# Moving a pair of second products behind scores and P@V in a fused attention and feed-forward kernel, with weights loaded in fewer slots

## The chip, the cores and the metric

One core of a Trainium2 chip. The time is device microseconds of one execution, median of several runs. PE is TensorE, DVE is VectorE, ACT is ScalarE, POOL is GpSimd, SP is SyncE; PEld is PE's weight load.

## What is computed

```python
scores = scale * np.matmul(q, k.transpose(0, 1, 3, 2))      # q, k, v: (8, 8, 576, 64)
kth = np.partition(scores, -32, axis=-1)[..., -32:-31]
scores = np.where(scores >= kth, scores, -1e9)
attn = np.exp(scores - np.max(scores, axis=-1, keepdims=True))
attn = attn / (np.sum(attn, axis=-1, keepdims=True) + 1e-09)
x = np.matmul(attn, v)                                       # then (B, H, S, D) -> (4608, 512)
h = x @ w_in                                                 # w_in (512, 2048)
out = (h * np.cos(h)) @ w_out                                # w_out (2048, 512)
```

Attention in which each query keeps its 32 largest scores, then a feed-forward layer over all 4608 tokens.

## The kernel before

**Units, blocks, slots.** A unit is 128 query rows of two heads (`hp`); there are 144. Four units (`NP = 4`) make a block of 128 tokens; there are 36 blocks, and block 4, 13, 22 and 31 lie across two batches. The main loop (L814) runs one slot for each unit. In slot i, VectorE searches the top 32 of unit u = i; ACT masks and exponentiates unit w = i-1; unit x = i-2 is split in halves, written to DRAM and read back transposed; every fourth slot z is the block whose P@V is due. I call slots by i modulo 4: slot 0 to slot 3.

**Attention.** `scores` (L229) makes the score products of a unit on PE, 448 columns in a bank of their own (`sc`, two buffers) and 128 in a shared tile `rim`. `take_scores` (L244) copies them out on ACT (L246, L250). `fold_high` (L252) is VectorE's maximum of the two halves of a row into `rest`; the minima `low` come from POOL by a sum and a difference (`fold_sum` L270 with L274, `fold_low` L278 with L283), or, for units listed in `BUSY`, from VectorE (`fold_now` L262, L266). `search` (L348) is MAX8 (L350) and MATCH_REPLACE8 (L355): four rounds on `rest`, two on `low`. `merge_first`, `merge_second`, `bounds` and `distances` (L333 to L372) give `nd` and the mask's bound, early in the next slot. `mask` (L374: L377, L379) and `exponentials` (L383: L387) run on ACT. `split` (L405: L410, L412) is POOL's, `write_halves` (L436) and `transposes` (L440) are DMAs of SP's queue. `values` (L453, L469) is P@V: 80 instructions of PE into `rim`, for four units in slot 2, or two in slot 0 and two in slot 2 for a block across two batches. `take_values` (L475, L481) normalizes them into `xT` on VectorE, in the middle of round 3; it waits for ACT's L250, which waits for P@V, since all three touch `rim`.

**Feed-forward.** First products (`ff1` L514, L530): w_in in four chunks of 512 columns (w_in0 to w_in3), each filling one PSUM bank with 16 matmuls; an item of kind 0 is half a chunk. `take_first` (L542) empties a bank on ACT (L544, L546). POOL reduces the argument (L566, L575), ACT takes the sine (L585), POOL gates (L592). Second products (`ff2` L595, L605): w_out0 to w_out15 of the block before, summed in one bank; an item of kind 1 is a pair. `take_second` (L613: L615, L617) takes that bank on ACT and stores it. Both kinds share two banks (tag `mm`): while an output sum is open, one bank is left, so a chunk of first products waits until the chunk before it was taken. `can_first` and `can_second` (L622, L632) hold an item back until its inputs were made enough ticks ago. `take_banks` (L552) issues what is due on ACT.

**The order.** Instructions are issued in the order in which the code calls them, and each engine runs its own in that order. `plan` (L717) says for each slot of four what `feed` (L648) hands PE at three places of `slot` (L724):

```python
        feed(*plan[i % NP][0])
        for m in made: scores(m)
        if z: values(z)
        ...                     # sines, mask, take_banks, exponentials, take_scores
        topk_round(u, 3, both(w), z)
        ...
        feed(*plan[i % NP][1])
        take_banks()
        ...
        feed(*plan[i % NP][2])
```

Scores are made in even slots, two units at a time. So a block's PE order from slot 2 is: w_out0-1, scores, P@V, w_out2-3; slot 3: w_in0, w_out4-7, half of w_in1; slot 0: its other half, scores, w_out8-11, half of w_in2; slot 1: its other half, w_out12-15, w_in3. The w_in are of the block whose `xT` slot 2 made, the w_out of the block before.

**Weights.** They come encoded, in 32 chunks of 512 KB, through staging buffers (`load_weights` L103): n in a slot, on SP's queue up to slot 5, on ACT's after. A chunk is decoded by ACT (L133, L136), VectorE (L144) and POOL (L154), in the slot after it lands or later. When all slots are done, `drain` and `forward` (L775 to L803) finish the last blocks with `feed_any` (L654).

Of the kernel before, what the change touches and what calls it, by code (L numbers as in the profile page):

```python
# [30 lines left out]
def kernel(  # L31
# [16 lines left out]
    NP = H // 2  # L48
# [43 lines left out]
        w_out.append(w)  # L92
        chunks.append((moe_w_out[f * P : (f + 1) * P, :], w))
    CHUNKS, XB = 6, 3
    BUSY = range(8, 11)
    ff = {"live": 0, "tick": 0, "now": 0, "end": False, "kind": 0, "half": 0, "open": 0, "late": False}

    wq = {"next": 0, "loaded": deque(), "second": deque(), "third": deque(), "done": 0, "ready": 0}
# [4 lines left out]
    def load_weights(n, queue):  # L103
        for _ in range(n):
            i = wq["next"]
            if i >= len(chunks):
                return
            src, dst = chunks[i]
            if not DECODE:
                queue.dma_start(out=dst, in_=src)  # L110
                wq["next"] = wq["done"] = i + 1
                continue
            spare = i < 2 * NC + 10 and i % 2 == 1 and staged(1) < XB
            if spare:
                st = ffw.tile([P, CW, 2], I32, tag="x", name="st", bufs=XB)
            elif staged() + ff["live"] >= CHUNKS:
                return
            else:
                st = ffw.tile([P, CW, 2], I32, tag="g", name="st", bufs=CHUNKS)
            queue.dma_start(out=st.rearrange("p w i -> p (w i)"), in_=src)  # L120
            wq["loaded"].append((st, dst, int(spare)))
            wq["next"] = i + 1
# [16 lines left out]
    def decode_second(n):  # L139

        for _ in range(min(n, len(wq["second"]))):
            st, w, spare = wq["second"].popleft()
            wi = w.bitcast(I32)
            nc.vector.tensor_scalar(  # L144
                out=wi, in0=wi, scalar1=3, scalar2=None, op0=ALU.logical_shift_left
            )
            wq["third"].append((st, w, spare))

    def decode_third():

        while wq["third"]:
            st, w, _ = wq["third"].pop()
            wi = w.bitcast(I32)
            nc.gpsimd.tensor_tensor(out=wi, in0=wi, in1=st[:, :, 0], op=ALU.add)  # L154
            wq["done"] += 1
# [96 lines left out]
    def fold_high(u):  # L252

        s, sc = u["s"], u["sc"]
        if u["n"] not in BUSY:
            del u["sc"]
# [5 lines left out]
    def fold_now(u):  # L262

        s, sc = u["s"], u.pop("sc")
        u["low"] = work.tile([P, 2, HS], F32, tag="low", name="low", bufs=1)
        nc.vector.tensor_tensor(  # L266
            out=u["low"], in0=sc[:, :, 0:HS], in1=s[:, :, HS:S], op=ALU.min
        )

    def fold_sum(u):  # L270

        s = u["s"].bitcast(I32)
        u["low"] = work.tile([P, 2, HS], F32, tag="low", name="low", bufs=1)
        nc.gpsimd.tensor_tensor(  # L274
            out=u["low"].bitcast(I32), in0=s[:, :, 0:HS], in1=s[:, :, HS:S], op=ALU.add
        )

    def fold_low(u):  # L278

        if u["n"] in BUSY:  # L280
            return
        low = u["low"].bitcast(I32)
        nc.gpsimd.tensor_tensor(  # L283
            out=low, in0=low, in1=u["rest"][:, :, HS:S].bitcast(I32), op=ALU.subtract
        )
# [15 lines left out]
    def topk_first(u, w):  # L301

        u["top"] = tops[u["n"] % len(tops)]
        if w:
            merge_first(w)
        if u["n"] not in BUSY:
            fold_sum(u)
        fold_high(u)
        if w:
            merge_second(w)  # L310
        if u["n"] in BUSY:
            fold_now(u)
        topk_round(u, 0, [lambda: bounds(w), lambda: distances(w)] if w else ())

    def topk_round(u, rnd, between=(), ahead=None):
        top, rest, lasts = u["top"], u["rest"], TOPK // 8 - 1
        end = TOPK - 1 - 8 * rnd
        at = top[:, :, end : end - 8 if rnd < lasts else None : -1, 0]
        search(
            at, rest[:, :, HS:S] if rnd == 0 else rest[:, :, 0:HS], rest[:, :, 0:HS], rnd < lasts,  # L320
            between if rnd < lasts else (),
        )
        if rnd < lasts:
            return
        del u["rest"]
        low = u.pop("low")
        for k in range(TOPK // 16):
            more = k < TOPK // 16 - 1
            if ahead and not more:
                take_values(ahead)  # L330
            search(top[:, :, 1 + 8 * k : 9 + 8 * k, 1], low, low, more, () if more else between)
# [3 lines left out]
    def merge_first(u):  # L335
        n = TOPK // 2 + 1
        u["lesser"] = u["top"].rearrange("p j r i -> p j (r i)")[:, :, 2 * n : 3 * n]
        nc.vector.tensor_reduce(
            out=u["lesser"], in_=u["top"][:, :, 0:n], axis=mybir.AxisListType.X, op=ALU.min
        )  # L340

    def merge_second(u):
        nc.vector.tensor_reduce(
            out=u["top"][:, :, TOPK - 1, 1], in_=u.pop("lesser"), axis=mybir.AxisListType.X,
            op=ALU.max,
        )
# [55 lines left out]
    def both(u):  # L402
        return [lambda: sums(u), lambda: reciprocal(u)] if u else ()
# [148 lines left out]
    def take_banks():  # L552
        while full:
            take, *what = full.popleft()
            take(*what)

    def reduce_first():

        if not fresh or (ff["late"] and not ff["end"] and fresh[0][4] == ff["now"]):
            return  # L560
        g, x = fresh[0][1:3]
        fresh[0][3] = True
        if ff["end"]:
            nc.vector.tensor_tensor(out=x, in0=g, in1=x.bitcast(I32), op=ALU.subtract)
            return
        nc.gpsimd.tensor_scalar(  # L566
            out=x, in0=x.bitcast(I32), scalar1=1.0, scalar2=0.0, op0=ALU.mult, op1=ALU.add
        )

    def reduce_second():  # L570
        if not fresh or not fresh[0][3]:
            return
        blk, g, x, *_ = fresh.popleft()
        if not ff["end"]:
            nc.gpsimd.tensor_tensor(out=x, in0=g, in1=x, op=ALU.subtract)  # L575
        waiting.append((blk, g, x, ff["now"]))

    def sines(least):

        n = sum(c[3] < ff["now"] for c in waiting)  # L580
        if n == 0 or (n < least and waiting[0][3] + 2 > ff["now"]):
            return
        for _ in range(n):
            blk, g, x, _ = waiting.popleft()
            nc.scalar.activation(out=x, in_=x, func=AF.Sin, bias=halfpi, scale=TWO_PI_BELOW)  # L585
            sined.append((blk, g, x))
# [61 lines left out]
    def feed(*kinds):  # L648

        ff["tick"] += 1  # L650
        for kind in kinds:
            item(kind)
# [43 lines left out]
    for n in range(NP, len(order)):  # L696
        i = last[order[n - 6]] if n >= 6 else 0
        load_at(max(i, 2 * NP + 2), load_qk, *order[n])
        i = last_values[order[n - 6]] if n >= 6 else 0
# [11 lines left out]
    def send(x):  # L711
# [3 lines left out]
        transposes(x)  # L715

    plan = (  # L717
        ((0,), (1,), (1, 0)),
        ((0,), (1, 1), (0, 0)),
        ((1,), (1,), ()),  # L720
        ((0, 0), (1, 1), (0,)),
    )

    def slot(i, u, w, x, z):  # L724
        n = (3, 4, 4, 4, 4, 3)[i] if i < NP + 2 else 2
        if i < NP:
            for load, b, hp in at_once[i]:
                load(b, hp)
        load_weights(n, nc.sync if i < NP + 2 else nc.scalar)
        if x:  # L730
            (turn if i < NP + 2 else send)(x)
        decoding = i < 3 * NP
        ff["late"] = False
        topk_first(u, w)
        fold_low(u)
        topk_round(u, 1)
        topk_round(u, 2)
        decode_second(NP)
        decode_third()
        reduce_first()  # L740
        reduce_second()
        made = scored.get(i, [])
        if z:
            take_banks()
        feed(*plan[i % NP][0])

        for m in made:
            scores(m)
        if z:
            values(z)  # L750


        if i % 2 or decoding:
            sines(1)
        if w:
            mask(w)
        take_banks()
        if w:
            exponentials(w)
        if i + 1 < NU:  # L760
            take_scores(units[i + 1])
        topk_round(u, 3, both(w), z)
        ff["late"] = True
        if i in at_slot:
            load, b, hp = at_slot[i]
            load(b, hp)
        gate(1)
        feed(*plan[i % NP][1])
        take_banks()
        decode_first(NP)  # L770
        reduce_first()
        reduce_second()
        feed(*plan[i % NP][2])
# [90 lines left out]
```

## Time and profile before

| what | us |
|---|---|
| median of 3 runs (1445.33 to 1447.82) | 1445.59 |
| the profiled execution | 1449.18 |
| its span, first to last instruction | 1447.4 |
| PE busy (95%) | 1374.4 |
| DVE busy (93%) | 1351.3 |
| POOL busy (80%) | 1164.8 |
| ACT busy (75%) | 1088.4 |
| first products, L530: 4608 instructions, 275 ns each | 538.7 |
| second products, L605: 1152, 602 ns each | 534.4 |

The mean granted clock of PE is 0.974; it is below 1 in the first 130 us and 1.00 in the stretches after it. Busy time of PE counts passes: a matmul of f32 shows as several instructions, so one pair of second products is "x4" in the chain, a chunk of first products "x32" (some records can be missing), and the lengths there, not the counts, are to be read. The chain of waits goes from the last instruction back to what released it; a "piece" is a run of the same engine and line.

### The profile page before, as it was taken

What the parts mean: (1) busy time and instruction counts of PE and PEld (TensorE: products, weight loads), DVE (VectorE), ACT (ScalarE), POOL (GpSimd) and SP (SyncE); (2) the same over time, 40 slices, a digit from 0 to 9 for tenths busy, and PEclk for the clock granted to TensorE, in tenths of its full rate; (3) what the DMA queues carried; (4) which work ended last, traced back from release to release, by engine and by line L of the source; (5) the groups of instructions that cost most, each with busy time, mean ns of one, the idle gap of its engine ahead of it and who ended that gap; (6) DMA issues with size and microseconds to landing.
All of it is one profiled execution on the core that took longest, in us unless ns stands there. A gap on an engine that the chain in (4) does not pass through costs nothing.

```text
span 1447.4 us, 30339 instructions
## 1 busy us (share of the span) xinstructions
PE 1374.4 (95%) x10304; PEld 991.8 (69%) x10304; DVE 1351.3 (93%) x5235; ACT 1088.4 (75%) x1922; POOL 1164.8 (80%) x804
## 2 busy tenths in 40 slices
PE   5558999999999999999999999999999999999998
PEld 3345777777777767777777767777777776777775
DVE  7998999999999999999999999999999999999931
ACT  7876777777777777877777777777777787777742
POOL 4877888888888888888888888888888888888820
PEclk6678999999999999999999999999999999999999
DMA  9596676666665667657666566656656566555640
GB/s 292 184 190 170 183 201 170 153 170 184 162 178 149 156 179 185 165 149 189 169 171 152 145 182 183 172 153 167 191 167 169 138 168 161 161 153 153 147 106 15
DMA packets 427436, 240.01 MB, mean 166 GB/s; under 512 B 375952, under 2 KB 392592, under 8 KB 427280
## 3 DMA queue, kind: packets, MB, share of 16 engines
q1 hardware_dynamic: 420720, 224.22, 58.7%
q10 hardware_dynamic: 6560, 13.85, 2.9%
q8 instruction: 81, 1.33, 0.4%
q14 instruction: 75, 0.61, 0.2%
HBM read 45.09 MB, written 101.19 MB: 101 GB/s over the span
## 4 chain that ended last, share of the span: by engine, by line
PE 41%; DVE 40%; ACT 14%; DMA 2%; issue 2%; POOL 1%; SPq 0%; ACTq 0%
DVE top L350 19%; PE o L605 14%; PE rim L469 11%; PE mm L530 10%; DVE rest L355 10%; PE sc L236 5%; DVE rest L258 4%; DVE low L355 3%; ACT s L379 3%; ACT L387 2%; ACT s L387 2%; DVE xT L481 2%; ACT s L246 1%; PE rim L236 1%; ACT s L250 1%
## 5 line engine op out<-in xcount | busy, mean ns | idle before, releaser
L530 PEld LDWEIGHTS mm<-xT,w_in 128*128 128x128 f32 x4608 | 537.7, 192 | 67.5 <-issue 51.6
L605 PE MATMUL o<-w_out,g 128*128 128x512 f32 x1152 | 534.4, 602 | 24.2 <-POOL g L592 10.5
L530 PE MATMUL mm<-xT,w_in 128*128 128x128 f32 x4608 | 538.7, 275 | 0.0
L350 DVE MAX8 top<-rest 128x8 f32<-128x288 f32 x1152 | 478.9, 451 | 0.0
L410 POOL COPY halves<-s 128x2304 uint16<-128x2304 uint16 x140 | 294.8, 2106 | 102.6 <-ACT s L387 98.7
L355 DVE MATCH_REPLACE8 rest<-top,rest 128x288 f32<-128x288 f32 x864 | 376.5, 443 | 0.0
L605 PEld LDWEIGHTS o<-w_out,g 128*128 128x128 f32 x1152 | 205.2, 190 | 230.2 <-issue 210.8
L350 DVE MAX8 top<-low 128x8 f32<-128x288 f32 x576 | 241.7, 449 | 0.0
L387 ACT ACTIVATE s<-s,nd 128x576 f32<-128x576 f32 x288 | 220.1, 766 | 0.8
L283 POOL TENSOR_TENSOR low<-low,rest 128x576 int32<-128x576 int32 x141 | 199.4, 1414 | 11.1
L379 ACT ACTIVATE s<-s,top 128x576 f32<-128x576 f32 x288 | 205.5, 761 | 0.0
L274 POOL TENSOR_TENSOR low<-s 128x576 int32<-128x576 int32 x141 | 198.8, 1410 | 5.9 <-ACT s L250 5.9
L575 POOL TENSOR_TENSOR x<-g,x 128x1024 f32<-128x1024 f32 x68 | 161.2, 2371 | 5.7
L377 ACT ACTIVATE nd<-nd 128x2 f32<-128x2 f32 x144 | 29.3, 204 | 176.1 <-DVE nd L370 176.0
L592 POOL TENSOR_TENSOR g<-g,x 128x1024 f32<-128x1024 f32 x68 | 161.0, 2367 | 0.0
L236 PE MATMUL sc<-k,q 64*128 64x448 f32 (+1 forms) x640 | 148.3, 584 | 12.4 <-DMA k<-in_k_dram 7.4
L469 PE MATMUL rim<-pT,v 128*64 128x128 f32 (+1 forms) x2560 | 140.5, 268 | 0.0
L469 PEld LDWEIGHTS rim<-pT,v 128*64 128x64 f32 x2560 | 130.3, 139 | 6.9 <-issue 5.8
L250 ACT COPY s<-rim 128x256 f32<-128x256 f32 (+1 forms) x160 | 59.4, 371 | 97.3 <-PE rim L469 97.1
L246 ACT COPY s<-sc 128x896 f32<-128x896 f32 x144 | 127.8, 888 | 3.0 <-PE sc L236 3.0
L355 DVE MATCH_REPLACE8 low<-top,low 128x288 f32<-128x288 f32 x288 | 125.4, 443 | 0.0
L544 ACT ACTIVATE g<-mm 128x512 f32<-128x512 f32 x144 | 84.8, 589 | 42.1 <-PE mm L530 31.0
(54 smaller groups left out, 1281.4 us busy)
## 6 DMA issues: line engine op xcount, KB each, us to landing
rows<-halves SPq DMA_DIRECT2D x140, 640.0 KB, 3.0
out_dram<-ob ACTq DMA_DIRECT2D x36, 256.0 KB, 2.1
q<-in_q_dram SPq DMA_DIRECT2D x31, 288.0 KB, 3.4
st<-in_moe_w_in_dram SPq DMA_DIRECT2D x16, 512.0 KB, 7.3
v<-in_v_dram SPq DMA_DIRECT2D x32, 256.0 KB, 3.3
k<-in_k_dram SPq DMA_DIRECT2D x31, 144.0 KB, 3.3
k<-in_k_dram SPq DMA_DIRECT2D x32, 128.0 KB, 3.4
st<-in_moe_w_out_dram SPq DMA_DIRECT2D x8, 512.0 KB, 4.4
```

What stands on the lines that cost most here:

```text
L236: nc.tensor.matmul(to[r0 : r0 + rows, rim_bank(r0, j) if k0 else place(u["hp"], j), 0 : k1 - k0], st["q"][d, q0 : q0 + rows], st["k"][d, k ...
L274: nc.gpsimd.tensor_tensor(out=u["low"].bitcast(I32), in0=s[:, :, 0:HS], in1=s[:, :, HS:S], op=ALU.add)
L283: nc.gpsimd.tensor_tensor(out=low, in0=low, in1=u["rest"][:, :, HS:S].bitcast(I32), op=ALU.subtract)
L350: nc.vector.max(to[:, j], src[:, j])
L355: nc.vector.match_replace(rest[:, j], to[:, j], src[:, j], NEG)
L379: nc.scalar.activation(out=s[:, j], in_=s[:, j], func=AF.Prelu, bias=less[:, j, 1:2], scale=1.0, alpha=FAR)
L387: nc.scalar.activation(out=s[:, j], in_=s[:, j], func=AF.Exp, bias=nd[:, j : j + 1], scale=SCALE, accum_out=den[:, j, 0:1],)
L410: nc.gpsimd.tensor_copy(out=halves[:, :, 0 : 2 * S], in_=s.rearrange("p (k h) -> p h k", h=2))
L469: nc.tensor.matmul(to[d, r], lhsT, rhs, start=(bank, j) not in begun, stop=c == NT - 1 and u in us[-2:] and r0 + rows == P,)
L530: nc.tensor.matmul(mm[:, at : at + w], w_in[f // FC][:, c, (f % FC) * P : (f % FC + 1) * P], blk["xT"][:, c], start=c == 0, stop=c == NC - 1,)
L575: nc.gpsimd.tensor_tensor(out=x, in0=g, in1=x, op=ALU.subtract)
L605: nc.tensor.matmul(o, g[:, at : at + P], w_out[f], start=f == 0, stop=f == NF - 1)
```

## The change

`BUSY` has unit 8 alone instead of 8, 9 and 10: for units 9 and 10 POOL makes the minima. From slot 6 on three weight chunks are loaded in a slot instead of two, as far as staging buffers are free; the last is loaded in slot 8 instead of slot 9. `plan` has the same sixteen items in four slots, one place later: PE's order from slot 2 becomes half of w_in3, scores, P@V, w_out0-1; slot 3: w_out2-3, w_in0, w_out4-7; slot 0: w_in1, scores, w_out8-11; slot 1: w_in2, w_out12-15, half of w_in3. In that order of PE alone, one pair (w_out0-1) goes from ahead of scores and P@V to behind; against ACT's instructions the halves of chunks move as well, as `feed`'s three places lie ahead of and behind the mask, the exponentials and `take_scores`.

```diff
-    BUSY = range(8, 11)
+    BUSY = (8,)
...
     plan = (
-        ((0,), (1,), (1, 0)),
-        ((0,), (1, 1), (0, 0)),
-        ((1,), (1,), ()),
-        ((0, 0), (1, 1), (0,)),
+        ((0, 0), (1,), (1,)),
+        ((0,), (0, 1), (1, 0)),
+        ((0,), (1,), ()),
+        ((1, 0), (0, 1), (1,)),
     )
 
     def slot(i, u, w, x, z):
-        n = (3, 4, 4, 4, 4, 3)[i] if i < NP + 2 else 2
+        n = (3, 4, 4, 4, 4)[i] if i <= NP else 3
```

## The prediction

> **What bounds the kernel now.** I read the page's chain by engine first: PE 41% and DVE 40%, so neither alone. Then the table of stretches, for two blocks of the steady part and for one earlier stretch; columns are the stretch, its length, busy time of PE, PEld, DVE, ACT, POOL, the granted clock, DMA share, GB/s.
>
> ```profile
> 155.00:200.00 45.00, 43.46 (x369) 30.40 (x370) 44.23 (x173) 35.73 (x65) 39.42 (x28) 1.00 0.71 194
> ...
> 348.00:386.00 38.00, 37.57 (x278) 27.12 (x276) 37.22 (x147) 29.47 (x53) 32.75 (x24) 1.00 0.66 174
> ```
>
> In 38 us PE is idle 0.43 us and VectorE 0.78 us. Two engines this full, each with a small hole, are tied into one loop. The waits name the holes (from engine and line, to releaser: total, times, longest):
>
> ```profile
> DVE xT L481 <- ACT s L250: 34.5, 33, 6.3
> PEld o L605 <- POOL g L592: 10.7, 1, 10.7
> PE o L605 <- ACT ob L615: 9.0, 21, 0.4
> PEld mm L530 <- ACT x L546: 7.2, 26, 0.4
> ```
>
> The chain of waits, in order of time over one block (start, us, what), shows the loop:
>
> ```profile
> 315.66 0.89 DVE xT L481 x4
> ...
> 337.23 0.02 issue
> 337.25 0.20 ACT nd L377
> 337.45 1.33 ACT s L379 x2
> 338.78 0.48 ACT g L544
> 339.27 0.58 ACT x L546
> ...
> 342.78 0.79 ACT s L246
> 343.57 0.27 ACT s L250
> 343.84 0.51 ACT ob L615
> 344.35 0.14 issue
> 344.49 1.95 PE o L605 x4
> 346.44 0.95 PE sc L236 x4
> ```
>
> After it come the rest of the scores (to 348.59), 4.26 us of P@V, 0.42 of L250 with its issue gaps, and the next xT at 353.28. So VectorE runs 21.59 us from xT to the `nd` of slot 1; ACT masks, takes chunk 2's bank (L544, L546), loads a table, makes exponentials, copies the next scores and takes the output bank, 7.24 with the issue; PE does the first pair 1.95, scores 2.15, P@V 4.26. The sum is 37.6, and xT repeats every 37.62 us. This length sets the time, not an engine's work: PE's is 37.2 a block, VectorE's 36.84.
>
> **The steady part, step by step.** In the program's order the pair of w_out0 and w_out1 moves from ahead of scores and P@V to behind. That takes 1.95 and the take of `ob` (0.51, and 0.14 issue) out of the loop. But what now stands right ahead of scores is chunk 3's products (w_in3, 16 matmuls). Two banks carry these products; while an output sum is open, the first products have one, so chunk 3's first matmul must wait until ACT has emptied chunk 2's bank (L546). Before, the same wait is in the list (PEld mm, 26 times, at most 0.4), because ACT took that bank ahead of slot 1's exponentials. The new plan splits chunk 2: its second half is issued after slot 1's `take_scores`, so L544 and L546 stand behind the table load, the exponentials, L246 and L250 on ACT. ACT is in order, and it can't start slot 1 before `nd`.
>
> So the new loop is: VectorE 21.59; ACT from `nd` to the end of L546: 7.24 less `ob` 0.51 less issue 0.14 = 6.59 (L544 and L546 moved inside it, 1.06 either way); PE's start after a release, 0.14 by the `ob` row; chunk 3, 3.57 (steady groups of 32 passes in the chain), and 0.15 as a group after a wait runs longer (a pair 1.95 against 1.72 to 1.91 in flow); scores 2.15; P@V 4.26; L250 0.42. Sum 38.87, or 38.7 without the 0.15. I take 38.8: **+1.2 us a block**. VectorE's wait at xT grows from 0.78 to about 2.0, and PE gets a hole of about 1.6 ahead of chunk 3. The other engines have room: POOL 32.75 and ACT 29.47 of 38.
>
> Other takes of banks move too. Chunk 0's goes behind slot 3's exponentials: its L546 ends 10.2 us after xT starts; PE reaches chunk 1 about 10.2 after it too (P@V's end, 0.42 earlier, + four products 3.6 + chunk 0 3.57 + four products 3.44). No path from there is longer: from chunk 1 to chunk 3 are 3.57 + 2.2 + 3.5 + 3.57 + 3.44 = 16.3, in all 26.6, against 28.3 by way of slot 1. Chunk 3's take goes ahead of slot 2's exponentials; ACT waited 2.79 there for P@V, which covers 1.06.
>
> From block 1's xT (126.6) to slot 142's there are 33 loops. Four pairs of them (a block of two batches) have P@V halves in slots 0 and 2: each half is 2.71, so slot 2's part is 1.55 shorter and PE sets 75.4 us for the pair; by the same sums I get 77.0. So 25 x 1.2 + 4 x 1.6 = **+36.4 us**.
>
> **The start.** Eight w_out chunks (512 KB) are issued from ACT's queue, in slots 6 to 9 before, in 6 to 8 now; each brings its decode (ACT 0.68 + 0.67, VectorE 0.36 to 0.5, POOL 1.27) one slot sooner. Rows of before (the chain):
>
> ```profile
> 97.70 15.80 DMA st<-in_moe_w_out_dram
> 115.56 4.82 DMA pT<-rows
> 120.43 5.77 PE rim L469 x68
> ```
>
> The last chunk took 15.8 us among the transposes; `rows` of unit 7, issued at 104.8, landed only at 115.5, its transpose at 120.4, and VectorE lost 6.3 at xT. With the last chunk issued near 89 (when POOL frees its buffer), I give rows the usual 3.6 and the transpose 4.9: pT near 114, P@V (no longer behind the pair that waited 10.5 for POOL's gate) ends near 119.5. The cover ends elsewhere: units 9 and 10 lose L266 on VectorE (2 x 0.75) and give POOL four folds of 1.41. POOL's queue in slots 9 and 10 (three L154 3.8, gate 2.4, halves 2.5, folds) frees unit 10's `low` near 119.4, where VectorE arrives at 117; queued behind that wait are two MAX8, two MATCH_REPLACE8 and xT, which starts near 121 instead of 126.6. **-5.6**; the ends are -9 (no wait for POOL) and 0 (the transposes as crowded as before). Half of block 0's chunk 0 ahead of slot 6's scores is idle PE time (0.5 busy there): nothing. SP's queue has the same instructions. An issue on ACT's queue (0.33) that waits for POOL to free its buffer holds up the next mask behind it; the third of slot 6 would wait until 69.3, and that mask waits for `nd` until 71.2 anyway.
>
> **The drain.** PE works without a hole from 1370.5 to the end. The pair now lies in it: +1.9. In the new order chunk 2 follows chunk 1 directly at one place, and must wait for ACT to take chunk 1's bank, 0.48 + 0.58 and two issues: +1.3. **+3.2**.
>
> **Sum.** 36.4 - 5.6 + 3.2 = +34.0. The profiled execution took 1449.18 (span 1447.4), so 1483.2 in its measure; it lies 3.6 above the median of the runs, and on the median, 1445.59, the sum gives 1479.6. I say **1479**.
>
> **A rule that makes it worse.** The stretches that I read from 130 us on show a granted clock of 1.00, through 21 holes of 0.4 and, at 193.7, one of 1.1. The Trainium skill, TensorE: Matmul & The Clock Gate, "A second HAM failure mode: psum-queue depth-cycling", says that short idle times of PE between groups, from cycling PSUM banks, can make the clock fall and rise again; its "HAM oscillation" section puts the limit at idle gaps over about 3.4 us. My estimate from that page's 3.4 us at half clock is 1.7 us a loop, some 56 us more, if holes of 1.6 us counted; by its limit they don't, and the sum is unchanged. No row of before has such a hole in every block.
>
> **Rivals.**
> - *PE sets the period (faster).* If chunk 2's bank is empty by the time PE has done w_out15, there is no hole; the loop has lost 2.6 and gained nothing, and PE's 37.2 decides: 25 x -0.43, the pairs 0, -5.6 + 3.2, in all -13: 1432.5. It needs ACT's L546 in slot 1 to end 1.6 us earlier than I place it. For it: PE and VectorE both have holes to close. Against it: the order on ACT, where `nd` at 337.25 and the rows behind it leave no gap.
> - *Even.* If that L546 ends 1.1 us earlier (table load and copies overlap more than their rows say), loops cost 0.1: +3 - 5.6 + 3.2, about 1446, no change.
> - *Worse.* The holes cost more than their length: releases of 0.4 instead of 0.14 (the longest wait of that kind), chunk 1 late behind chunk 0's take, POOL's backlog of the start kept: 0.5 a loop more, +17: 1496.
>
> **Chances.** Forecast 0.74, worse 0.11, even 0.05, faster 0.10. The forecast's own ends: 1.0 to 1.4 a loop (25 to 35, pairs 4 to 9), start 0 to -9, drain 1.9 to 4, so 1467 to 1494. The range must hold 8 in 10: 1464 to 1497. Slower by over 0.2% (what a measurement here can tell from no change): 0.85; within 0.2%: 0.05; faster: 0.10.
>
> **What would show it.** Right: xT every 38.8 us; VectorE's wait "xT <- ACT s L250" some 60 us in all; a wait of PE mm L530 for ACT x L546 of about 1.6 us in some 25 blocks; ACT ob gone from PE's waits; ACT nd L377 to x L546 in the chain, then PE mm x32 and scores. Start: xT of block 1 near 121, a wait of DVE `top` for POOL `low` of about 3 in all. Wrong: no PE wait for L546, or a period near 37.2.

## The result, and the profile after

The changed kernel takes 1489.56 us (median of 4 runs, 1488.87 to 1489.85); the kernel before, run beside it, 1445.46 (4 runs, 1443.44 to 1447.82). The ratio is 1.0304, 95% interval 1.0286 to 1.0322: **slower by 3%**, 44.1 us. The profiled executions differ by 40.3 (1489.5 against 1449.18), because the one of before lies 3.7 above its median and the one of after lies on its own.

The table of stretches, over a block of the steady part (the stretch, its length, busy time of PE, PEld, DVE, ACT, POOL, the granted clock, DMA share, GB/s):

```profile
350.00:389.00 39.00, 37.55 (x274) 26.86 (x272) 36.91 (x145) 29.25 (x52) 32.37 (x22) 1.00 0.58 162
```

PE and VectorE are busy as long as before in a longer block: PE's idle time in it grew from 0.43 to about 1.4 and VectorE's from 0.78 to about 2.1 us. The clock stayed at 1.00. The waits of the whole trace (engine and line, to releaser: total, times, longest) name both holes:

```profile
DVE xT L481 <- ACT s L250: 69.0, 37, 3.3
PE mm L530 <- ACT x L546: 53.6, 41, 6.1
```

PE's wait for L546 was at most 0.4 before, on its weight load; the wait of `o` for `ob` is gone from the list. The chain of waits shows the loop that holds them, from slot 1's `nd` to the next xT (start, us, what):

```profile
338.70 0.07 DVE nd L370
338.77 0.02 issue
338.79 0.20 ACT nd L377
339.00 1.33 ACT s L379 x2
340.33 0.02 issue
340.35 1.28 ACT L387
...
342.32 0.94 ACT s L387 x3
343.27 0.79 ACT s L246
344.06 0.10 ACT s L250
344.16 0.07 issue
344.22 0.60 ACT g L544
344.82 0.59 ACT x L546
345.41 0.04 issue
345.46 3.84 PE mm L530 x32
349.29 0.95 PE sc L236 x4
...
351.44 4.26 PE rim L469 x80
...
356.13 0.88 DVE xT L481 x4
```

Before, L544 and L546 stood between the mask and the table load (L387 alone is the load). Now they come last on ACT, chunk 3's 3.84 us of products start 0.04 after them, and only then scores and P@V. The xT before this one was at 317.20, so the loop takes 38.93. PE's timeline has the hole in brackets, ahead of chunk 3:

```profile
340.50 3.60 PE L605 MATMUL o<-w_out,g 128*128 128x512 f32 x8
345.46 3.84 PE L530 MATMUL mm<-xT,w_in 128*128 128x128 f32 x32 [1.36 <-ACT x L546]
```

Where the time went, by the xT of block 1, the end of slot 142's P@V and the end of the span, in the two profiled executions: start 126.63 to 122.08, so -4.5; loops 1243.8 to 1285.3, so +41.4; drain 76.9 to 80.35, so +3.4. The sum is +40.3. How much of the start's -4.5 holds for an ordinary execution is taken up below. An ordinary block is 38.93 against 37.62; the two blocks at a batch's border take 77.18 against 75.00.

### The profile page after: what moved, and what is told of

Its sections match the earlier page's. It is cut to its first block, busy times and chain, and to the rows that moved or that the text cites. A ratio compares the mean times of both kernels' runs of the same rounds, so it can differ in the third digit from the quotient of the medians.

```text
span 1487.7 us, 30363 instructions
## 1 busy us (share of the span) xinstructions
PE 1380.3 (93%) x10304; PEld 988.8 (66%) x10304; DVE 1351.3 (91%) x5233; ACT 1092.4 (73%) x1922; POOL 1170.8 (79%) x808
## 4 chain that ended last, share of the span: by engine, by line
DVE 48%; PE 32%; ACT 15%; issue 2%; POOL 1%; DMA 1%; SPq 0%; POOLq 0%
DVE top L350 23%; PE mm L530 12%; DVE rest L355 11%; PE rim L469 10%; PE o L605 5%; DVE rest L258 4%; PE sc L236 4%; DVE low L355 4%; ACT s L379 3%; ACT L387 3%; ACT s L387 3%; DVE xT L481 2%; ACT s L246 2%; ACT x L546 1%; ACT g L544 1%
## 5 line engine op out<-in xcount | busy, mean ns | idle before, releaser
L530 PE MATMUL mm<-xT,w_in 128*128 128x128 f32 x4608 | 546.4, 277 | 56.7 <-ACT x L546 53.6
L605 PE MATMUL o<-w_out,g 128*128 128x512 f32 x1152 | 524.9, 599 | 0.0
L387 ACT ACTIVATE s<-s,nd 128x576 f32<-128x576 f32 x288 | 220.5, 769 | 0.8
L566 POOL TENSOR_SCALAR x<-x 128x1024 f32<-128x1024 int32 x68 | 71.0, 1045 | 93.9 <-ACT x L546 93.9
L250 ACT COPY s<-rim 128x256 f32<-128x256 f32 (+1 forms) x160 | 59.5, 372 | 100.7 <-PE rim L469 100.5
L246 ACT COPY s<-sc 128x896 f32<-128x896 f32 x144 | 128.3, 891 | 2.6 <-PE sc L236 2.4
```

Of the source, the lines that this page charges most:

```text
L387: nc.scalar.activation(out=s[:, j], in_=s[:, j], func=AF.Exp, bias=nd[:, j : j + 1], scale=SCALE, accum_out=den[:, j, 0:1],)
L530: nc.tensor.matmul(mm[:, at : at + w], w_in[f // FC][:, c, (f % FC) * P : (f % FC + 1) * P], blk["xT"][:, c], start=c == 0, stop=c == NC - 1,)
L605: nc.tensor.matmul(o, g[:, at : at + P], w_out[f], start=f == 0, stop=f == NF - 1)
```

## The experiments

**The theory**: the cost is one place in ACT's order. Chunk 2's take (L544, L546, which empty its bank) stands behind slot 1's exponentials and `take_scores`; as chunk 3 has only that bank, this puts chunk 3 into the loop. **Rivals**: the moved pair itself costs (A); the minima on POOL or the loads cost (B); ACT's or PE's load as such.

All runs in one table. "Loop" is an ordinary block from xT to xT, "pair" the two at a batch's border, "block 1" the start of block 1's xT, all in us and of the profiled execution. Each ratio is to runs of the kernel before made beside it (medians 1444.67 to 1445.46).

| run | median us | ratio to before | block 1 | loop | pair |
|---|---|---|---|---|---|
| before | 1445 | 1 | 126.63 | 37.62 | 75.00 |
| after | 1489.56 | 1.0304 (1.0286 to 1.0322) | 122.08 | 38.93 | 77.18 |
| early_take | 1444.94 | 0.9999 (0.9991 to 1.0008) | 121.72 | 37.32 | 76.42 |
| mid_take | 1455.92 | 1.0076 (1.0060 to 1.0091) | 121.36 | 37.85 | 76.09 |
| pair_only | 1423.97 | 0.9861 (0.9847 to 0.9874) | 118.66 | 36.96 | 74.88 |
| twice_c2 | 1540.86 | 1.0664 (1.0649 to 1.0679) | 121.36 | 39.57, 41.19 | 78.38 |
| early_both | 1425.63 | 0.9867 (0.9854 to 0.9881) | 121.56 | 36.96 | 74.87 |
| half_c2 | 1503.37 | 1.0405 (1.0390 to 1.0421) | 121.13 | 39.35 | 77.96 |
| loads_only | 1450.53 | 1.0041 (1.0029 to 1.0054) | 127.77 | 37.62 | 75.01 |
| pair_loads | 1426.65 | 0.9874 (0.9860 to 0.9889) | 123.57 | 36.97 | 74.86 |
| plan_only | 1488.21 | 1.0304 (1.0289 to 1.0319) | 119.94 | 38.93 | 77.19 |
| pair_twice | 1427.45 | 0.9887 (0.9863 to 0.9911) | 121.83 | 36.95 | 74.89 |
| pair_three | 1427.83 | 0.9882 (0.9867 to 0.9896) | 123.19 | 36.95 | 74.87 |
| pair_busy5 | 1424.29 | 0.9858 (0.9843 to 0.9873) | 120.24 | 36.96 | 74.86 |

**early_take**: against the kernel after, slot 1's row of the plan:

```diff
-        ((0,), (0, 1), (1, 0)),
+        ((0, 0), (1, 1), (0,)),
```

> The kernel after with one row of the plan changed: slot 1 becomes (0, 0), (1, 1), (0,). PE's order is the same in every instruction; on ACT chunk 2's take (L544, L546) goes from behind the table load, the exponentials, L246 and L250 of slot 1 to ahead of them. Theory (the place of that take on ACT is the cost, the pair's move is not): chunk 3 no longer waits for L546, the loop by way of ACT and PE is 38.93 - 3.84 (chunk 3) = 35.1, under PE's own work of about 37.2 a block, so PE sets the period: 25 blocks x -1.73 and 4 pairs x -2.15, in all -52, so about 1438 (1430 to 1444), below both kernels. Rival A (the moved pair, which PE's order alone holds, is the cost): the time stays at 1489. Rival B (POOL with the minima of units 9 and 10, or the loads, carry the loss): stays within 5 of 1489.

1444.94: rivals A and B fall, since 44.6 us go with PE's order, loads and minima unchanged. But it isn't the 1438 of the theory: the loop is 37.32, longer than PE's own work (36.95, see pair_only), and a pair at a border gained 0.76 instead of 2.15. The chain of waits shows why, in slot 3 (start, us, what):

```profile
320.02 0.27 ACT s L250
320.29 0.50 ACT g L544
320.79 0.59 ACT x L546
321.38 0.04 issue
321.42 3.84 PE mm L530 x32
```

These are chunk 0's take, behind slot 3's exponentials, and chunk 1 waiting for it: the same form in another place, hidden until the first was gone. PE stands idle for only 0.1 there; the rest is chunk 1 itself, which takes 3.84 after the wait instead of 3.57.

**mid_take**: early_take's row, and slot 1's take held back to stand between the exponentials and L246:

```diff
-        take_banks()
+        if i % NP != 1 or i < 3 * NP:
+            take_banks()
         if w:
             exponentials(w)
+        take_banks()
```

> As early_take, but slot 1's take of chunk 2 is issued between the exponentials and L246: L246 and L250 alone change sides with it, from the kernel after. Theory: L546 ends 0.79 + 0.10 and an issue gap of 0.07 earlier, the loop is 38.93 - 0.95 = 38.0; 25 blocks and 4 pairs x -0.95 = -28, so about 1462 (1457 to 1467), a bit over half way back. The hole of PE ahead of chunk 3 shrinks from 1.36 to about 0.4. Rival A: 1489. If the table load and the exponentials were not in the way and only the copies were: the full gain, 1438.

1455.92, just under the range expected, and the loop 37.85 against 38.0: the effect is as the theory has it, a bit larger. By the chain of waits L546 comes not only 0.95 sooner (L246, L250 and their gap); L544 and L546 also take 1.06 here and 1.19 in the kernel after. PE's hole is 0.28:

```profile
339.20 3.84 PE L530 MATMUL mm<-xT,w_in 128*128 128x128 f32 x32 [0.28 <-ACT x L546]
```

**pair_only**: against the kernel before, slot 2's row alone:

```diff
-        ((1,), (1,), ()),
+        ((), (1, 1), ()),
```

> The kernel before with slot 2's row of the plan as (), (1, 1), (): the pair w_out0-1 goes behind scores and P@V, and nothing else: chunks keep their places against ACT's instructions, minima and loads stay as before. Theory: the pair 1.95 and the take of ob 0.65 leave the loop (37.6 to 35.0), nothing comes in, and PE's work decides, 37.2 a block: 25 x -0.43 = -11, drain +2, so about 1437 (1433 to 1443), faster. Rival A (the pair behind P@V is the cost): near 1489, or at least slower than 1450.

1423.97, 1.4% under the kernel before: the move of the pair, by itself, is a gain, and a larger one than expected. The page's chain by engine, and a block in the table of stretches:

```profile
PE 92%; DVE 3%; ACT 2%; DMA 2%; POOL 0%; SPq 0%; issue 0%; POOLq 0%; ACTq 0%
```

```profile
306.00:343.00 37.00, 37.00 (x274) 27.06 (x273) 36.89 (x146) 29.20 (x52) 32.33 (x24) 1.00 0.72 198
```

In this block PE has no hole at all, and the loop is 36.95, not the 37.2 that I took from busy time (a chunk after a wait reads 3.84, in flow 3.57, so busy time of a block with waits is too long). From block 1's xT to slot 142's P@V the run takes 19.3 less than before, where 11 was expected. The rest is in the start: block 1's xT comes 8.0 sooner than in before's profiled execution, some 4 of which are left on the medians.

**twice_c2**: against the kernel after, L544 twice for chunk 2 (`twice` is true there alone):

```diff
-        nc.scalar.mul(out=g[:, at], in_=mm, mul=INV_2PI / UP)
+        for _ in range(1 + twice):
+            nc.scalar.mul(out=g[:, at], in_=mm, mul=INV_2PI / UP)
```

> The kernel after with L544 issued twice for chunk 2 (the same values are written twice): one ACT instruction of about 0.60 more in slot 1, behind L250 and ahead of L546. Theory: all of it stands in the loop: +0.60 to +0.62 a block, 25 blocks and 4 pairs of two: +18 to +21 with every loop counted, so about 1508 (1505 to 1512). Rival (ACT, which is busy 29 of 39 us, has room for it): within 2 of 1489.

1540.86, +51.3, where the theory said +18 to +21. ACT has no room for it, so the rival falls, but the theory lacks something. The loops are of two lengths. Those of 39.57 show the added instruction alone, +0.64. The others are 41.19; in those, PE's timeline shows chunk 3 at 5.47 instead of 3.84:

```profile
310.52 5.47 PE L530 MATMUL mm<-xT,w_in 128*128 128x128 f32 x32 [1.99 <-ACT x L547]
...
351.72 3.84 PE L530 MATMUL mm<-xT,w_in 128*128 128x128 f32 x32 [1.98 <-ACT x L547]
```

and the table of stretches, cut fine around both (the granted clock is the third number from the end), says what it is:

```profile
310.50:314.00 3.50, 3.48 (x16) 3.48 (x17) 3.50 (x15) 2.00 (x4) 3.10 (x3) 0.51 0.65 262
...
351.50:355.00 3.50, 3.28 (x29) 3.28 (x30) 3.50 (x16) 2.19 (x5) 3.18 (x3) 1.00 0.92 270
```

The clock was granted at half for 3.41 us after some of the holes, 19 times between the start and the drain (a twentieth spell lies at the very end, behind the work). 19 x 1.62 = 31, and the instruction itself gives 25 x 0.64 + 4 x 1.2 = 21: together 52, which covers the 51.3.

**half_c2**: the kernel after, with one more L544 over half of chunk 2's columns (`more` is true there alone):

```diff
+        if more:
+            nc.scalar.mul(out=g[:, half * 512 : half * 512 + 256], in_=mm[:, 0:256], mul=INV_2PI / UP)
```

> The kernel after with L544 issued once more for 256 of the 512 columns of chunk 2: about half of the doubled instruction's 0.62, so a hole of PE of about 1.36 + 0.3 = 1.66 instead of 1.99. Theory of the loop alone: +0.3 a block, about +9, 1499 (1496 to 1502), granted clock 1.00 in every stretch. With the doubled one the clock was at half for 3.41 us twenty times, and the blocks with it were 41.19 instead of 39.57. Rival (every hole longer than 1.36 can set the clock back): some of those spells here as well, +1.6 each, 1505 to 1530.

1503.37, 1.4 above the range expected. The loop is 39.35: the added instruction cost 0.42, not 0.3, and all of it counts. Holes of 1.77 and 1.78 set no clock back:

```profile
346.98 3.84 PE L530 MATMUL mm<-xT,w_in 128*128 128x128 f32 x32 [1.77 <-ACT x L548]
```

One hole between the start and the drain did, one of the four longer ones (1.95 to 1.96) at the batches' borders:

```profile
544.37 5.47 PE L530 MATMUL mm<-xT,w_in 128*128 128x128 f32 x32 [1.95 <-ACT x L548]
```

**early_both**: against the kernel after, slots 1 and 3:

```diff
-        ((0,), (0, 1), (1, 0)),
+        ((0, 0), (1, 1), (0,)),
         ((0,), (1,), ()),
-        ((1, 0), (0, 1), (1,)),
+        ((1, 0, 0), (1,), (1,)),
```

> The kernel after with two rows of the plan changed: slot 1 as (0, 0), (1, 1), (0,) and slot 3 as (1, 0, 0), (1,), (1,). PE's order is the same in every instruction; chunk 2's take and chunk 0's take both go ahead of the exponentials on ACT. Theory (two takes behind exponentials, each with a chunk of PE waiting for it, one hidden by the other): no hole of PE in a block, xT every 36.95 as when the pair alone was moved, against 38.93: 25 x -1.98, 4 pairs x (74.9 - 77.2), in all -59, so about 1431 (1427 to 1435); start and drain as in the kernel after. Rival (the remaining loss of early_take, 1445 against 1424, comes from minima and loads): 1445, xT every 37.3.

1425.63, a little under the range expected, and the loop 36.96, that of pair_only, where PE has no hole: with both takes ahead of the exponentials the change's 44 us of loss come back and 19 more, with nothing moved on PE. This closes what early_take left open.

**loads_only** and **pair_loads**: the other part of the change, on the kernel before and on pair_only:

```diff
-    BUSY = range(8, 11)
+    BUSY = (8,)
...
-        n = (3, 4, 4, 4, 4, 3)[i] if i < NP + 2 else 2
+        n = (3, 4, 4, 4, 4)[i] if i <= NP else 3
```

> The kernel before with the other part of the change alone: minima of units 9 and 10 by POOL, three chunks a slot from slot 6 on. By the prediction's working of the start it gains there: -3 to -5.6, so about 1441 (1439 to 1443). Rival (the gain of the start is the pair's, which no longer stands ahead of P@V with its wait for POOL's gate: xT of block 1 came at 118.7 when the pair alone was moved, 126.6 before, 122.1 after): nothing or a loss by POOL's folds, 1445 to 1449.

> The kernel before with the pair moved (slot 2 as (), (1, 1), ()) and the minima and loads of the kernel after: what is left of the change when no chunk changes its place against ACT. If the loads gain in the start: 1424 less 3 to 5, about 1420. Rival (as above, the loads and POOL's folds lose there, xT of block 1 at 122 instead of 118.7): 1424 plus 3, about 1427.

1450.53 and 1426.65: it loses 5.8 on the one and 2.7 on the other; the prediction's gain isn't there. The loops are as without it, so the loss is in the start.

**pair_three**: pair_only with the new loads, the minima left with VectorE.

> The kernel before with the pair moved and three chunks a slot from slot 6 on, minima of units 9 and 10 still by VectorE: it parts the 2.7 that loads and minima cost together. If POOL's four folds of 1.4 (they stand in the chain of the run with both, L274 and L283 up to 111.9, then VectorE) are the loss: 1424, or 1 to 2 less by the earlier loads. If the loads are the loss (three decodes of POOL in slot 8 and 9, 3.8, ahead of L566 and the halves): 1427.

1427.83, as with both: the loads lose, POOL's folds don't. The chains of waits of pair_only

```profile
90.85 0.07 DVE nd L370
90.91 0.02 issue
90.94 0.20 ACT nd L377
...
113.36 4.69 PE rim L469 x80
```

and of pair_three

```profile
85.92 1.30 POOL w_out L154
87.24 0.60 ACT g L544
...
90.99 0.58 ACT w_out L133
...
93.79 0.56 ACT st L136
94.35 0.08 ACT nd L377
...
117.44 5.30 PE rim L469 x80
```

show where: the mask of slot 8 is 3.4 late, and P@V 4.1. The third decode of slot 7 (1.1) is the lesser part: ACT sat idle for 3.0 ahead of that mask in pair_only, and `nd` itself is 2.5 late here (93.25 against 90.76 on VectorE's timeline), so the decodes hold up the mask by 0.9 only. The larger part stands ahead of the decodes. Chunk 0's take in slot 7 had waited 5.0 for a decode on POOL, and the exponentials and `take_scores` stand behind it on ACT; VectorE waits for them, 1.5 and 0.3, ahead of `nd` (ACT's timelines, pair_only's line first):

```profile
81.96 0.57 ACT L544 ACTIVATE g<-mm 128x512 f32<-128x512 f32 x1
87.24 0.60 ACT L544 ACTIVATE g<-mm 128x512 f32<-128x512 f32 x1 [5.01 <-POOL w_out L154]
```

loads_only and pair_loads have the same wait (5.02 and 5.01); before, pair_only, plan_only and the kernel after don't have it. In the code `g` and most staging buffers share one pool of six (tag `g`), so it fits that the third load of slot 7 took the buffer that L544 needed, and POOL's decode gave it back; no run moved that buffer alone.

**plan_only**: the kernel after with the minima and loads of before.

> The kernel after with the minima and loads of the kernel before: the plan alone. The prediction's working of the start (loads gain 3 to 5.6) would make it 1493 to 1495. What the two runs of the loads show (5.8 lost on the kernel before, 2.7 lost with the pair moved) would make it 1484 to 1487; loops and drain as in the kernel after, xT every 38.93.

1488.21 (1486.93 to 1491.62) against 1489.56: no gain by the loads and minima, and a loss smaller than I expected, not told from nothing. In the kernel after the new loads go 3, 2, 3 in slots 6 to 8, as a chunk begun ahead of slot 6's scores already holds a buffer, while on the plan of before they go 3, 3, 2. So in the kernel after slot 7 has two decodes, L544 doesn't wait there for POOL, and the mask of slot 8 isn't late.

**pair_twice**: pair_only with twice_c2's doubled instruction.

> The kernel before with the pair moved, and L544 issued twice for chunk 2, the same instruction that cost 51 us in the kernel after. Theory: chunk 2's take stands ahead of slot 1's exponentials, PE has no hole, and its bank is empty long before PE has done w_out12-15; the loop by way of scores and P@V (35.0) grows by 0.6 and stays under PE's 36.95. So nothing: 1424 (1422 to 1426), xT every 36.95. Rival (ACT's time as such counts): +18 to +20, 1443.

1427.45 (1425.97 to 1432.79), above the range expected. The loop is 36.95, so in an ordinary block the instruction that cost 0.64 and a clock spell costs nothing. The 3.5 us lie elsewhere: block 1's xT is 3.2 later, and of three stretches of eight blocks with a border two take 0.55 more (297.51 against 296.96). Why the start is later was not tried.

**pair_busy5**: pair_only with `BUSY = range(8, 13)`.

> The kernel before with the pair moved and two units more on VectorE's minima (8 to 12): takes four POOL folds of 1.4 out of slots 11 and 12 and puts 2 x 0.7 on VectorE there, where PE has just got its first full blocks. If POOL still holds up the second block (xT of block 2 at 156.8, 38.1 after block 1's, against 36.95 later): about 1 less, 1423. If VectorE does: 1 to 1.5 more, 1425.

1424.29: no difference from pair_only. Neither expectation is borne out: from 120 to 200 us PE is idle for 0.9 in pair_only and for 0.1 here, so PE is all but the bound there already.

## Why the prediction was right, point by point

- **What bounds the kernel**: right. It is a loop; the loop's length follows each change of what stands ahead of L546 on ACT (37.85, 38.93, 39.35, 39.57 where no clock spell falls).
- **The steady part, +1.2 a block**: right in mechanism, measured 1.31. From `nd` to L546's end 6.64, predicted 6.59; PE's start 0.04, predicted 0.14; chunk 3 after the wait 3.84, predicted 3.57 + 0.15. This last term is the mis-sized one, besides taking 38.8 for the 38.87 of the sum. PE's hole is 1.36, predicted about 1.6.
- **The pairs at a border, +1.6 each**: 2.18. Over 25 blocks and 4 pairs the two make the 41.4 against 36.4.
- **"No path from there is longer"**, on chunk 0's take and chunk 1: right; its 26.6 against 28.3 said that it would be next, 1.7 behind, and early_take found it 1.6 behind (37.32). I left it out of early_take's expectation.
- **The start, -5.6**: -4.5 between the two profiled executions, but only about -0.7 on the medians (see the sum below), and not for the reason given. The step gave it to the earlier loads and to P@V no longer standing behind the pair. The second half holds: against before's profiled execution the pair alone makes block 1's xT 8.0 earlier and the plan alone 6.7 (about 3.7 less each on the medians). The first half fails: the loads lose 2.7 to 5.8 with the plans of before and pair_only, and with the new plan the loads and minima gain nothing; plan_only, which issues the last chunk at 97.6, has block 1's P@V at 113.8, the kernel after, which issues it near 90, at 115.3. The step that failed is to have given the third load of a slot no price but that of its own issue: with the plan of before chunk 0's take then waits 5.0 for POOL, `nd` comes 2.5 later, and the decodes (0.68 + 0.67 each), counted as free, hold up the mask by another 0.9. Why nothing is gained with the new plan, where this wait is absent, stays open. POOL's folds were placed rightly: VectorE waits for `low` once, 1.8 (predicted about 3), and xT comes at 122.1 (predicted 121).
- **The drain, +3.2**: +3.4, with the bank's wait where it was put (the chain of waits, start, us, what). pair_only's drain, which has the pair without this wait, is 1.7 longer than before's (predicted 1.9).

```profile
1425.69 1.80 PE mm L530 x16
1427.48 0.02 issue
1427.51 0.60 ACT g L544
1428.10 0.59 ACT x L546
1428.69 0.04 issue
1428.73 2.05 PE mm L530 x16
```

- **The sum on the median**: the sum was +34.0 on the profiled execution, measured +40.3; I then took off the 3.6 by which that execution lay above its median. After's profiled execution doesn't lie above its own, so these 3.7 are a second part of the miss. Most likely they lie in before's start: loads_only, whose profiled execution lies on its median, has before's plan and the same loops (1243.7) and drain (76.9). By 44.1 - 41.4 - 3.4 the change then moves the start by about -0.7 on the medians, so that -4.5 came near the predicted -5.6 was luck of that one execution. Which part of the start it is, was not tried.
- **The rival "PE sets the period"**: its condition, chunk 2's bank empty in time, is what early_both and pair_only meet. Its price of 1432.5 was 7 to 8.5 us too high: the loops in all shrink by 19 to 22 instead of 11, as PE's block is 36.95 instead of 37.2 and the block ahead of a border falls from 38.79 to about 37.3.
- **The clock rule**: the holes of 1.36 left the clock at 1.00, as the sum had it; see below for how near the edge that was.

## What to carry to other kernels

Two orders count, not one: the same order on PE costs 1489.6 or 1425.6 us, by where ACT's take of a bank stands against its long instructions. Ask of every bank that is reused at once which instructions stand ahead of its release on the releasing engine, and what that engine waits for first. When a loop is shortened, work out the next longest one in the same sum. What a changed start brings has to be followed on each engine's own queue and in each pool of buffers: an earlier transfer takes a buffer earlier, and whoever needed that buffer waits.

## What the runs showed of the hardware

- **A clock that falls at short holes.** In an ordinary block PE had one hole, of 1.36 (after), 1.77 (half_c2) or 1.98 to 1.99 us (twice_c2). With the first two the granted clock stayed at 1.00. In twice_c2 it went to half 19 times, for 3.41 us each, at a cost of 1.62: after 17 of the 21 holes of 1.98 to 1.99, two of the four of 2.17 and none of the four of 1.94 to 1.95, which lie at borders. In half_c2 one of the four holes of 1.95 to 1.96 did it. Spells one block apart start 40.96 us apart, which is 12 x 3.41, and all 19 starts lie on one grid of 3.413 us, within the 0.02 to which they can be read. Laid over the holes (half_c2's by its one spell), this grid tells which count: every one of the 20 spells follows a hole that lies whole within the one stretch of the grid ahead of it (308.53 to 310.52 in the stretch 307.19 to 310.60, say), and a line of the grid cuts every hole of 1.94 or more that set nothing back (349.74 to 351.72, cut at 351.57). The closest of these ends 0.01 behind its line, less than can be read; in all the others the longer piece is at most 1.93. In half_c2 holes of 1.76 to 1.78 that lay whole in a stretch set nothing back. So in these runs the clock is judged by fixed stretches of 3.41 us, and about 1.95 us of unbroken idle time in one of them is what it took; 1.78 never did it, nor did the one piece of 1.93. The Trainium skill, TensorE: Matmul & The Clock Gate, "HAM oscillation — how this bites in real kernels", asks for no idle gap of PE over about 3.4 us; here gaps of 1.95 were enough, and the measurement decides. The same page, "What's actually happening", gives a free-running window of 3413 ns, which agrees with the length of the spells.
- **A chunk after a wait is longer**: 16 f32 products of 128x128 read 3.84 us after a hole of any length from 0.1 to 1.98 at full clock, and 3.57 in flow.
- **A release by ACT reaches PE in 0.04** in every chain above; before, the `ob` row had 0.14.
